# X's decays from half the lags, an immediate cosine bias, first steps of u in row pairs, and projections dealt over thirteen places a group

## The chip, the cores and the metric

The kernel runs as one program on one core of a Trainium2 chip. The metric is the device time of one execution in microseconds (us); for the kernel before it was taken three times. Below, PE is the matmul engine, ACT the scalar engine, DVE the vector engine, POOL the GpSimd engine, and SP the engine that issues most of the DMA transfers.

## The reference

Two branches over L = 2048 positions and D = 448 channels are mixed by a gate, all in f32.

```python
# A: a state space model's kernel of 2048 lags, applied to u as a convolution
dt = exp(log_dt);  A = -exp(log_A_real) + 1j * A_imag;  C = (C_real + 1j * C_imag) * dt
K = 2 * einsum("dn,dnl->dl", C, exp(A * dt * l)).real          # 256 states n, 2048 lags l
a = irfft(rfft(u, 2 * L) * rfft(K, 2 * L))[:L] + u * D_skip
# B: attention in 4 segments of 512 with a memory M, z; 16 heads of 28
q, k, v = x @ wq, x @ wk, x @ wv
for s in range(4):
    a_dot = softmax(q_s @ k_s.T * scale + mask) @ v_s
    a_mem = phi(q_s) @ M / (phi(q_s) @ z)
    o_s = sigmoid(beta) * a_mem + (1 - sigmoid(beta)) * a_dot
    M += phi(k_s).T @ v_s;  z += sum(phi(k_s))
b = concat(o) @ wo
out = g * a + (1 - g) * b,   g = sigmoid((x * gate_w).sum(-1)),  x = u
```

## The kernel before, in words

The program has three stretches: a preparation, a first half and a second half. The edit lies in the first two; the second half (attention, the Fourier steps, the output) keeps its instructions.

**Preparation** (`prepare_params`). The parameters lie as tiles of 112 rows (a quarter of the channels, four `j` side by side) by 256 states. Decay rates and phases are cut into three bf16 parts each (`parts`) and go to DRAM (SD, SP), from where `load_decay` and `load_phase` fetch them for four channels at a time into one of five tiles `lh`. `cab`, a factor of each channel and state, is brought with the states on the partitions by eight PE transposes.

**First half** (`first_half`). The kernel K is computed in 28 steps J of 16 channels, two steps to a *group*, so fourteen groups. A lag is split into a high part of 32 values and a low part of 64; the terms exp(-decay * lag) are therefore products of EX (high lags, 32 for each channel) and EY (low lags, 64 for each channel), and the same holds for the turning phases. For each J, `decay` makes three tiles: a pair of matmuls (two row halves of the array, one for each half of the states) writes the exponents to PSUM (`ps_arg`), and ACT takes the exponential of 1024 columns: two tiles EY and one EX. POOL then multiplies EX by `cab` (`scale`). For each half step n (four in a group), `turns(n)` writes the phases to PSUM with eight matmuls, `trig(n)` makes sine and cosine on ACT with three instructions (Sin, Abs, and Sin of the Abs with a bias of pi/2 read from the tile `bhp`), `product(n)` makes X and Y on DVE with four multiplications, and `sums(n)` contracts them with 64 small matmuls into `ps_k`. Sines and exponentials need different tables on ACT: each group has one table load ahead of its four sine blocks and one ahead of its decays. `decays(g + 1)` stands at the end of group g, and `sums` of a group's last half step is done within it.

**What is worked in between.** The class `Feed` holds a generator (`project`) of the projections q, k and v for branch B with their weight splits, stores and feature maps. The first half calls `feed.spend(us)` at five places: four lumps of `1.7 * RATES[g]`, one after each `trig(n)`, and after the tiles of `decays` by `PLACE` times `RATES[g]`. `spend` adds to a debt, at most 4.0, and takes steps from the generator until the debt is paid. When a step yields "pe", its products are held until the next decay, since their exponentials need that table: `exps` releases them ahead of a decay's exponential. A second generator, `transform_u`, does the first of the Fourier steps on u: 32 steps of one matmul on half of the rows (64), an eviction and a store. `project` takes steps from it (`filling`) at fixed places, and so does `spend` where a debt stays.

**The weight splits.** `weights` in `project` handles eight tiles of wq and wk (`win`): ACT copies the tile into the first half of a tile `wsp` as rounded values, POOL subtracts to get the rest, SP stores both to DRAM (WD). Two tiles `wsp` of their own are used in turn. A projection unit later fetches its weights from WD into a tile `w` (`load_w`), of which there are two.

The order of instructions on each engine follows from the program order of these calls and from a scheduler that simulates the engines; a change in one place can so shift others.

## Time and profile before

| | us |
|---|---|
| median of three runs | 871.44 |
| lowest and highest run | 870.67 and 874.49 |
| span of the profiled execution | 866.7 |
| preparation, up to the first table load for sines | 57.58 |
| first half, fourteen groups | 390.42 |
| second half | 418.70 |
| busy in the first half: PE, ACT, DVE, POOL | 347.50, 340.27, 295.22, 63.54 |

The page gives for the profiled execution its span alone, from the first to the last instruction; the times of the runs are a little longer than that span. The stretches are cut where ACT loads a table for a group's sines. The groups begin at 57.58, 89.28, 117.69, 144.63, 174.72, 200.49, 227.47, 254.69, 284.79, 310.56, 335.91, 363.23, 391.97 and 419.19 us, and the first score of the second half stands at about 448.

In the rows, a timeline's line gives the start, the duration, the engine, the line of the kernel, the operation, output<-inputs, the shape, how many instructions were joined (x), and in brackets the idle time before with what ended it. A window's line gives for each engine its busy time with its number of instructions, then the granted clock of PE (1.00 is full), the busy share of the DMA engines and GB/s. SPq is SP's DMA issue; line L1335 (L1337) is the helper through which most ACT instructions go, L1370 that of the matmuls.

### The profile page before, as it was taken

What the parts mean: (1) busy time and instruction counts of PE and PEld (TensorE: products, weight loads), DVE (VectorE), ACT (ScalarE), POOL (GpSimd) and SP (SyncE); (2) the same over time, 40 slices, a digit from 0 to 9 for tenths busy, and PEclk for the clock granted to TensorE, in tenths of its full rate; (3) what the DMA queues carried; (4) which work ended last, traced back from release to release, by engine and by line L of the source; (5) the groups of instructions that cost most, each with busy time, mean ns of one, the idle gap of its engine ahead of it and who ended that gap; (6) DMA issues with size and microseconds to landing.
All of it is one profiled execution on the core that took longest, in us unless ns stands there. A gap on an engine that the chain in (4) does not pass through costs nothing.

```text
span 866.7 us, 18996 instructions
## 1 busy us (share of the span) xinstructions
PE 753.7 (87%) x7575; PEld 410.3 (47%) x7597; DVE 596.9 (69%) x1160; ACT 539.2 (62%) x638; POOL 173.1 (20%) x217
## 2 busy tenths in 40 slices
PE   1687988998879988799979799999997998888997
PEld 1364655765547644476534444444443443343443
DVE  7988778777787777877648656656664747664564
ACT  4876989798997999979842255544453434431220
POOL 5224111001110011101100111222313124222110
PEclk9998999998999999999979689999999999878799
DMA  9347753334633255323569948557465545654873
GB/s 242 91 110 247 227 185 104 96 111 154 205 124 96 96 169 194 122 92 132 178 218 347 317 133 264 178 193 249 139 222 189 193 162 168 216 187 164 221 231 100
DMA packets 88290, 153.11 MB, mean 177 GB/s; under 512 B 20626, under 2 KB 57162, under 8 KB 88154
## 3 DMA queue, kind: packets, MB, share of 16 engines
q1 hardware_dynamic: 79130, 140.83, 50.2%
q10 hardware_dynamic: 7424, 9.18, 3.1%
q0 software_dynamic: 1648, 1.89, 0.7%
q8 instruction: 60, 0.98, 0.5%
q14 instruction: 28, 0.23, 0.1%
HBM read 90.87 MB, written 60.63 MB: 175 GB/s over the span
## 4 chain that ended last, share of the span: by engine, by line
PE 52%; ACT 16%; DVE 13%; issue 7%; DMA 7%; POOL 2%; SPq 1%; ACTq 0%; DVEq 0%; POOLq 0%
PE ps_a L1370 18%; PE ps_m L1370 16%; PE ps_pv L1370 7%; ACT cs L1335 7%; PE ps_arg L1370 4%; DVE jk L992 3%; PE ps_k L1370 3%; PE ps_m L1373 2%; ACT L1335 2%; DVE Y L397 2%; DMA WD<-wsp 1%; ACT EX L1335 1%; DMA dn<-pvs 1%; DVE Y L398 1%; DMA ident<-in_c_id 1%
## 5 line engine op out<-in xcount | busy, mean ns | idle before, releaser
L1023 ACT ACTIVATE PT<-ps_a 128x1024 f32<-128x1024 f32 (+1 forms) x96 | 84.5, 881 | 122.9 <-PE ps_a L1370 115.9
L992 DVE CUSTOM_DVE_ANT_0 jk<-ps_a,mk 128x512 f32<-128x512 f32 (+3 forms) x256 | 124.9, 488 | 49.6 <-PE ps_a L1370 42.3
L359 POOL TENSOR_TENSOR EX<-EX,cab 128x1024 f32<-128x1024 f32 x28 | 54.0, 1928 | 309.3 <-ACT EX L1335 286.3
L1335 ACT ACTIVATE cs<-ps_arg 128x1024 f32<-128x1024 f32 x111 | 107.3, 1021 | 2.7 <-DVE Y L398 2.4
L1370 PE MATMUL ps_a<-qu,ku 32*128 32x512 f32 (+3 forms) x768 | 92.9, 364 | 1.3 <-DVE mx L992 0.6
L1370 PE MATMUL ps_m<-xh,w 112*128 112x512 f32 x256 | 92.9, 412 | 0.7 <-DVE lo L762 0.5
L393 DVE TENSOR_TENSOR X<-EX,cs 128x1024 f32<-128x1024 f32 x56 | 70.5, 1260 | 23.2 <-ACT cs L1335 21.5
L1034 POOL TENSOR_SCALAR_AFFINE_SELECT PT<-PT 128x256 f32<-128x256 f32 (+1 forms) x96 | 47.1, 493 | 178.9 <-ACT PT L1023 178.7
L1370 PE MATMUL ps_k<-Y,X 128*32 128x64 f32 x3584 | 64.1, 226 | 11.8 <-DVE Y L398 11.8
L1370 PEld LDWEIGHTS ps_k<-Y,X 128*32 128x32 f32 x3584 | 54.9, 113 | 38.0 <-DVE Y L398 19.9
L397 DVE TENSOR_TENSOR Y<-EY,cs 128x1024 f32<-128x1024 f32 x56 | 70.0, 1251 | 0.0
L1370 PEld LDWEIGHTS ps_a<-qu,ku 32*128 32x128 f32 x768 | 64.8, 201 | 10.1 <-issue 3.2
L1335 ACT ACTIVATE cs<-cs,bhp 128x1024 f32<-128x1024 f32 x56 | 64.5, 1151 | 1.8
L1370 PE MATMUL ps_a<-ku,qu 32*128 32x512 f32 (+3 forms) x256 | 47.2, 404 | 16.0 <-DVE mx L992 8.4
L399 DVE SCALAR_TENSOR_TENSOR Y<-EY,cs 128x512 f32<-128x512 f32 x56 | 39.4, 704 | 30.5 <-ACT cs L1335 29.7
L1335 ACT ACTIVATE EY<-ps_arg 128x1024 f32<-128x1024 f32 x52 | 53.1, 1030 | 11.1 <-PE ps_arg L1370 10.0
L1370 PEld LDWEIGHTS ps_m<-xh,w 112*128 112x128 f32 x256 | 48.0, 188 | 20.0 <-issue 7.6
L1370 PEld LDWEIGHTS ps_a<-ku,qu 32*128 32x128 f32 x256 | 23.1, 195 | 62.7 <-issue 28.6
L1370 PE MATMUL ps_m<-xl,w 112*128 112x512 f32 x128 | 50.3, 393 | 0.0
L1370 PE MATMUL ps_arg<-ct,lh 64*128 64x512 bf16 x224 | 43.1, 386 | 8.1 <-ACT cs L1335 5.0
L1370 PEld LDWEIGHTS <-lh 64*128 64x128 bf16 x392 | 22.1, 95 | 50.6 <-issue 37.8
L604 DVE TENSOR_TENSOR pr<-ps_a,ks 128x896 f32<-128x896 f32 x32 | 34.7, 1085 | 15.7 <-PE ps_a L1370 15.4
(214 smaller groups left out, 1408.7 us busy)
## 6 DMA issues: line engine op xcount, KB each, us to landing
w<-WD SPq DMA_DIRECT2D x32, 448.0 KB
qu<-QD SPq DMA_DIRECT2D x16, 512.0 KB
ku<-KD SPq DMA_DIRECT2D x16, 512.0 KB
GU<-gs SPq DMA_DIRECT2D x32, 224.0 KB
GK<-gs SPq DMA_DIRECT2D x8, 896.0 KB
gk<-GK SPq DMA_DIRECT2D x32, 224.0 KB
gu<-GU SPq DMA_DIRECT2D x32, 224.0 KB
BB<-bs ACTq DMA_DIRECT2D x16, 448.0 KB
```

Source lines behind the costliest of these rows:

```text
L359: nc.gpsimd.tensor_tensor(o, o, cab, ALU.mult)
L393: v.tensor_tensor(X, ex, t[:, :, 0], ALU.mult)
L397: v.tensor_tensor(Y[:, :, :, :32], lo, y[:, :, :, ::-1], ALU.mult)
L398: v.tensor_tensor(Y[:, 0, :, 32:], ey[:, :, 32:], y[:, 0], ALU.mult)
L399: v.scalar_tensor_tensor(Y[:, 1, :, 32:], ey[:, :, 32:], -1.0, y[:, 1], ALU.mult, ALU.mult)
L604: nc.vector.tensor_tensor(pr[c], pt, ks.pop(c), ALU.mult)
L992: v.tensor_tensor_reduce(junk[:, :n], pt[:, x, o : o + n], k.mk[:, SEG - n :], 1.0, -3e38, ALU.add, ALU.max, mx[:, 3 - t, h : h + 1],)
L1023: nc.scalar.activation(PT[:, 2 * hp : 2 * hp + 2, 512 * b : 512 * b + n], pt[:, :, :n], AF.Exp, scale=SCALE)
L1034: nc.gpsimd.affine_select(sl, sl, pat, ALU.is_ge, 0.0, base=0, channel_multiplier=-1)
L1335: x = op(*args, **kw)
L1370: tc.keep_in_program_order(nc.tensor.matmul(*args, **kw))
L1373: tc.keep_in_program_order(nc.tensor.transpose(*args))
```

## The change

Five things are changed.

1. *X's decays.* `decay_x(J)` replaces two of the six `decay` calls of a group. It makes one tile ER for two steps J, from 16 high lags instead of 32 (256 columns for each J and half of the states), with four matmuls of 256 columns and one exponential of 1024. POOL's `scale` now writes EX from it in two multiplications of half the size: the first 16 lags are ER times `cab`, the other 16 are these times `gx` = exp(-1024 * decay). `gx` is prepared with eight transposes and two exponentials; so that the rates are still there, `parts` subtracts into a new tile `lr`. A group's decays start with `decay_x`, then come the four EY.
2. *Cosine's bias.* The bias pi/2 is an immediate instead of the tile `bhp`.
3. *u's first step.* When `k.pairs` is set, `transform_u` issues the two matmuls of a pair (upper and lower 64 rows) one after the other and then both evictions and stores.
4. *Dealing out.* `spend(g, share)` gives each of thirteen places of a group its share of `SHARES[g]`: five in the decays (PLACE) and eight in the sines (TRIG), two for each half step, one after `trig` and one after `sums`. The cap of 4.0 is gone, and releasing held exponentials no longer clears the debt. `FILLERS[g]` of u's steps, thirteen in all, are taken in pairs by a credit in `spend`; `project` takes none itself.
5. *Buffers.* The two tiles `wsp` now take the two buffers of the tag "w", which the tiles `w` use afterwards.

```diff
+    def decay_x(J):
+        pt = k.ps("arg")
+        for a in range(2):
+            for nt in range(2):
+                r, kw = rows(nt)
+                k.mm(
+                    pt[:, nt, 256 * a : 256 * a + 256], lt[J + a][r, 2], k.ce[r, 1024:],
+                    start=True, stop=True, **kw,
+                )
+        raw = gy.tile([128, 2, 2, 256], F32, tag="ER", name="ER", bufs=1)
+        exps(raw, pt)
+        for a in range(2):
+            EX[J + a] = raw[:, a]
+            if J > 0:
+                scale(J + a)
...
     def scale(J):
-        o = EX[J]
...
-            nc.gpsimd.tensor_tensor(o, o, cab, ALU.mult)
+        r = EX[J].rearrange("p t (d c) -> p t d c", c=16)
+        EX[J] = gy.tile([128, 2, 512], F32, tag="EX", name="EX", bufs=2)
+        o = EX[J].rearrange("p t (d c) -> p t d c", c=32)
+        lo, hi = 16 * J, 16 * J + 16
+        nc.gpsimd.tensor_tensor(o[:, :, :, :16], r, over(k.cab, lo, hi, 16), ALU.mult)
+        nc.gpsimd.tensor_tensor(o[:, :, :, 16:], o[:, :, :, :16], over(k.gx, lo, hi, 16), ALU.mult)
...
-        act(fl, fl, AF.Sin, bias=k.bhp, scale=-TWO_PI)
+        act(fl, fl, AF.Sin, bias=math.pi / 2, scale=-TWO_PI)
...
     def decays(g):
-        for J in (2 * g, 2 * g + 1):
-            for blk in range(3):
-                decay(J, blk)
-                if g > 0 and J % 2 and blk == 1:
-                    sums(4 * g - 1)
-                if g > 0:
-                    k.exps = 3 * (J % 2) + blk >= 2
-                    feed.spend(PLACE[3 * (J % 2) + blk] * RATES[g])
-                    k.exps = False
+        order = [(decay_x, (2 * g,))] + [(decay_y, (2 * g + a, blk)) for a in range(2) for blk in range(2)]
+        for i, (f, args) in enumerate(order):
+            f(*args)
+            if g > 0 and i == 3:
+                sums(4 * g - 1)
+            if g > 0:
+                k.exps = i >= 1
+                feed.spend(g, PLACE[i])
+                k.exps = False
...
         trig(n)
-        feed.spend(1.7 * RATES[n // 4])
+        feed.spend(n // 4, TRIG)
         product(n)
         if n == 2 * NJ - 1:
             feed.fill(2)
         if n % 4 > 0:
             sums(n - 1)
+        feed.spend(n // 4, TRIG)
...
-PLACE = (1.24, 0.62, 0.62, 0.62, 0.0, 0.62)
-RATES = (1.65, 1.65, 1.24, 1.55, 1.55, 1.17, 1.17, 1.48, 1.55, 1.17, 1.17, 1.48, 1.48, 1.65)
+PLACE = (0.9, 0.45, 0.45, 0.0, 0.45)
+TRIG = 0.5
+SHARES = (12.4, 11.6, 8.9, 15.2, 15.3, 8.1, 8.1, 14.5, 15.3, 8.1, 8.1, 14.5, 14.6, 12.8)
+FILLERS = (1, 0, 2, 0, 0, 2, 3, 0, 0, 2, 3, 0, 0, 0)
+SLOTS = sum(PLACE) + 8 * TRIG
...
-    def spend(self, us):
-        self.due = min(self.due + us, 4.0)
+    def spend(self, g, share):
+        part = share / SLOTS
+        self.due += SHARES[g] * part
+        self.credit += FILLERS[g] * part
         self.ends = False
         while self.due > 0 and not (self.held or self.done or self.ends and self.waiting):
             self.due -= self.step()
-        if self.due > 1.5 and (self.held or self.done) and self.waiting:
-            self.due -= next(self.filling, 0.0)
+        if self.credit > 0.99:
+            self.credit -= 1.0
+            self.k.pairs = True
+            next(self.filling, None)
+            self.k.pairs = False
     def exps(self):
         if self.held:
-            self.due = 0.0
             self.step()
...
-    wsp = [pp.tile([112, 4, 2, 4, 32], F32R, name=f"wsp{i}") for i in range(2)]
+    wsp = [
+        pp.tile([112, 4, 2, 128], F32R, tag="w", name="wsp", bufs=2).rearrange("p g b (j e) -> p g b j e", e=32)
+        for i in range(2)
+    ]
...
-    for _ in parts(k.SD, la, nc.gpsimd.tensor_tensor, k.pdma):
+    for _ in parts(k.SD, la, nc.gpsimd.tensor_tensor, k.pdma, new("lr", early)):
         pass
+    for nt in range(2):
...
+        nc.scalar.activation(by_j(k.gx[:, nt]), by_p(pt), AF.Exp, scale=-1024.0)
```

Three places of the programs show what the change moves. The first is ACT in group 0, from its table load on; `cs` are the sine tiles, `wsp` the copies of the weight splits, `win` their source. Before:

```order
L1337 ACT_TABLE_LOAD
L1337 ACTIVATE cs<-ps_arg 128x2x2x256
L1335 ACTIVATE cs<-ps_arg 128x2x2x256
L1335 ACTIVATE cs<-cs,bhp 128x1024
L1335 ACTIVATE wsp_212<-win 112x4x4x28
L1335 ACTIVATE cs<-ps_arg 128x2x2x256 x2
L1335 ACTIVATE cs<-cs,bhp 128x1024
L1335 ACTIVATE wsp_213<-win 112x4x4x28
L1335 ACTIVATE cs<-ps_arg 128x2x2x256 x2
L1335 ACTIVATE cs<-cs,bhp 128x1024
L1335 ACTIVATE wsp_212<-win 112x4x4x28
L1335 ACTIVATE cs<-ps_arg 128x2x2x256 x2
```

And now:

```order
L1378 ACT_TABLE_LOAD
L1378 ACTIVATE cs<-ps_arg 128x2x2x256
L1376 ACTIVATE cs<-ps_arg 128x2x2x256
L1376 ACTIVATE cs<-cs 128x1024
L1376 ACTIVATE wsp<-win 112x4x4x28 x2
L1376 ACTIVATE cs<-ps_arg 128x2x2x256 x2
L1376 ACTIVATE cs<-cs 128x1024
L1376 ACTIVATE wsp<-win 112x4x4x28 x2
L1376 ACTIVATE cs<-ps_arg 128x2x2x256 x2
L1376 ACTIVATE cs<-cs 128x1024
L1376 ACTIVATE wsp<-win 112x4x4x28 x2
L1376 ACTIVATE cs<-ps_arg 128x2x2x256 x2
```

The copies of group 0 stood one after each sine block, with the rest behind the table load for the decays; now they stand in pairs after the first, second and third block.

The second place is SP's queue in the same group, where `WD` is the DRAM tensor of the split weights and `w` a projection unit's weight tile. Before:

```order
L1394 DMA WD<-wsp_212 112x4x256
L1394 DMA win<-in_B_wk 112x448
L1394 DMA WD<-wsp_213 112x4x256
L1394 DMA win<-in_B_wk 112x448
L733 DMA w<-WD 112x1024 x2
L1394 DMA WD<-wsp_212 112x4x256
L328 DMA lh_91<-SP 48x2x128 x2
L1394 DMA WD<-wsp_213 112x4x256
```

And now:

```order
L1436 DMA WD<-wsp 112x4x256
L1436 DMA win<-in_B_wk 112x448
L1436 DMA WD<-wsp 112x4x256
L1436 DMA win<-in_B_wk 112x448
L1436 DMA WD<-wsp 112x4x256
L334 DMA lh_90<-SP 48x2x128 x2
L1436 DMA WD<-wsp 112x4x256 x3
L779 DMA w<-WD 112x1024 x3
```

The first two loads of `w` stood between the fourth and the fifth store of the splits; now all loads stand behind the eighth.

The third place is ACT from the table load for the decays in group 3 (it makes the decays of group 4), where `e` and `hi` are what was held of the projections. Before:

```order
L1335 ACT_TABLE_LOAD
L1335 ACTIVATE e<-ps_m 128x512
L1335 ACTIVATE hi<-ps_m 128x512
L1335 ACTIVATE e<-ps_m 128x512
L1335 ACTIVATE hi<-ps_m,po 128x512
L1335 ACTIVATE EY<-ps_arg 128x1024
L1335 ACTIVATE v_207<-ps_m 128x16x28
L1335 ACTIVATE EY<-ps_arg 128x1024
L1335 ACTIVATE EX<-ps_arg 128x1024
L1335 ACTIVATE EY<-ps_arg 128x1024 x2
L1335 ACTIVATE EX<-ps_arg 128x1024
```

And now:

```order
L1376 ACT_TABLE_LOAD
L1376 ACTIVATE ER<-ps_arg 128x2x2x256
L1376 ACTIVATE e<-ps_m 128x512
L1376 ACTIVATE hi<-ps_m 128x512
L1376 ACTIVATE e<-ps_m 128x512
L1376 ACTIVATE hi<-ps_m,po 128x512
L1376 ACTIVATE EY<-ps_arg 128x1024 x4
```

The two EX have become one ER, and it has moved from among the EY to the head of the decays, ahead of the held exponentials.

More of the change, by code (lines that the diff above doesn't have):

```diff
@@ L523, in transform_u @@
     uts = {0: load(0), 1: load(1)}
[L524 to L528 removed]
+    todo = [(w, h) for w in range(16) for h in range(2)]
+    while todo:
+        n = 2 if k.pairs and todo[0][1] == 0 else 1
+        now, todo = todo[:n], todo[n:]
+        pts = []
+        for w, h in now:
+            if h == 0 and w < 14:
+                uts[w + 2] = load(w + 2)
             pt = k.ps("m")
[L530 to L533 removed]
+            r = slice(64 * h, 64 * h + 64)
+            k.mm(pt[:, :D], k.s1u[r], uts[w][r], start=True, stop=True)
+            pts.append(pt)
+        for (w, h), pt in zip(now, pts):
             gs = up.tile([128, D], F32, tag="gs", name="gs", bufs=3)
@@ L1346, in gated_mix @@
     k.exps = False
+    k.pairs = False
     def copy(out, x, f, **kw):
```

90 lines of the change are left out of this document (39 added, 51 removed).

## The prediction

> **What bounds the kernel now.** I read the busy times first, then the span cut at the points where ScalarE (ACT) loads the table for a group's sines, then the timeline of single groups. Busy times of the page first, then groups 0, 1, 3, 9, 10 and 13 with the sum over all fourteen:
>
> ```profile
> PE 753.7 (87%) x7575; PEld 410.3 (47%) x7597; DVE 596.9 (69%) x1160; ACT 539.2 (62%) x638; POOL 173.1 (20%) x217
> ...
> core 0: us, PE busy (x) PEld busy (x) DVE busy (x) ACT busy (x) POOL busy (x), PEclk, DMA share, GB/s
> 57.58:89.28 31.70, 23.87 (x355) 13.97 (x358) 24.81 (x23) 23.70 (x26) 15.73 (x9) 0.89 0.76 226
> 89.28:117.69 28.41, 27.37 (x374) 17.60 (x372) 22.50 (x30) 24.08 (x26) 3.83 (x2) 1.00 0.75 246
> 144.63:174.72 30.09, 28.27 (x390) 20.06 (x387) 20.28 (x31) 24.48 (x28) 3.83 (x2) 1.00 0.24 73
> 310.56:335.91 25.35, 22.02 (x346) 13.17 (x346) 19.98 (x27) 24.43 (x28) 3.82 (x2) 1.00 0.51 171
> 335.91:363.23 27.32, 22.04 (x344) 13.07 (x345) 22.54 (x32) 26.00 (x32) 3.83 (x2) 0.94 0.42 141
> 419.19:448.00 28.81, 23.74 (x330) 12.38 (x329) 19.32 (x29) 19.51 (x25) 1.91 (x1) 0.89 0.45 157
> sum 390.42, PE 347.50 PEld 218.64 DVE 295.22 ACT 340.27 POOL 63.54; mean PE 24.82 PEld 15.62 DVE 21.09 ACT 24.31 POOL 4.54
> ```
>
> The whole-span shares hide the stage that is edited. The fourteen groups fill 57.58 to 448.00, 390.4 us of 866.7, and what follows them is the same program before and after. Taking group 0 and group 13 off the sum leaves twelve groups (89.28 to 419.19, 329.9 us) with PE busy 347.50 - 23.87 - 23.74 = 299.9 and ACT busy 340.27 - 23.70 - 19.51 = 297.1. So a group lasts 27.5, holds 25.0 of PE and 24.8 of ACT, and neither has more than 2.7 to spare. The rows show two kinds: 144.63 has PE at 28.27 of 30.09 while ACT waits, and 310.56 and 335.91 have ACT at 24.43 of 25.35 and 26.00 of 27.32 while PE waits. Group 0 is of a third kind: no engine is full, and it lasts 31.7.
>
> **The change, part by part.** *X's decays.* In each group two EX exponentials become one. The form rows of two tiles, a stretch of PE's timeline with a pair of decay products, and two rows of ACT's:
>
> ```profile
> L359 POOL TENSOR_TENSOR EX<-EX,cab x28: 1910/1912/2357, 60.0 to 419.2; 128x1024 f32<-128x1024 f32 x28
> L1335 ACT ACTIVATE EX<-ps_arg x26: 1007/1024/1032, 83.8 to 418.1; 128x1024 f32<-128x1024 f32 x26
> ...
> 163.15 0.39 PE L1370 MATMUL ps_arg<-ce,lh 64*128 64x512 bf16 x2
> 163.47 0.47 PE L1370 MATMUL ps_m<-wvh,xh 112*128 112x450 f32 x1
> ...
> 29.94 1.15 ACT L211 ACTIVATE pin_c<-pin_g,bhp 112x1024 f32<-112x1024 f32 x1
> 31.00 1.04 ACT L211 ACTIVATE pin_b<-pin_g 112x1024 f32<-112x1024 f32 x1
> ```
>
> ACT loses one exponential of 1.02, about 0.93 in a row of them since neighbours overlap by about 0.1 (29.94 + 1.15 against a next start at 31.00). PE loses half of two pairs of 512 columns; a pair holds PE from 163.15 to 163.47, so 0.32 a group. POOL does two multiplications of half the size for one of 1.91: the same 3.8 a group, or up to 4.5 if the halves carry a fixed cost.
>
> *Cosine's bias.* The same function on the same shape takes 1.15 with a bias tile and 1.04 without. Four cosines a group: 0.4 of ACT.
>
> *u's first step in pairs.* Two steps use the upper and lower 64 rows of the array.
>
> ```profile
> 123.73 1.02 PE L1370 MATMUL ps_m<-ut,s1u 64*128 64x448 f32 x2
> ```
>
> One step is two passes in 1.02, the last 0.2 of it overlapping what follows, so 0.8. The pair of decays above shows two row halves running in the time of one. Thirteen pairs in thirteen groups would give 0.8 each; some of the old steps already ran beside a decay's other half, so I take 0.65, with bounds 0 and 0.9.
>
> *The dealing.* In groups 1 to 12, then, ACT loses 0.93 + 0.4 = 1.3 and PE 0.32 + 0.65 = 1.0. A group ends by the later of two nearly equal engines, so the gain is about 1.0 to 1.3 if the 2.5 us of mutual waiting stay. Spreading the projections over eight places in the sines instead of four should take something off that waiting. Against it stands the new place of X's decay: it is the first exponential of a group, and PE reaches it only behind the third sums and a slice of projection. One group's decays in the timeline today:
>
> ```profile
> 217.57 1.28 ACT L1335 ACT_TABLE_LOAD   x1
> ...
> 217.88 1.10 PE L1370 MATMUL ps_k<-Y,X 128*32 128x64 f32 x64
> ...
> 218.87 0.60 ACT L1335 ACTIVATE e<-ps_m 128x512 f32<-128x512 f32 x1
> ```
>
> Today ACT fills that gap with the held exponentials (e at 218.87, right after the table load). Afterwards ACT waits for sums (to 218.9), about 0.7 of projection and 0.3 of decay: to 219.9, 1.0 late, which costs only where ACT is the bound. I take 1.25 a group net, -15 for twelve; bounds -2 (the waits only move) and -27 (1.3 and another 1.0 of waiting gone).
>
> *Group 0.* Six of the eight q and k weight splits fall here. Each goes ACT copy, POOL subtraction, store to DRAM, and a tile is free for its next copy when its store has landed. Now the copies go out in pairs after each sine block, and the tiles that the projections read their weights into share the two buffers of the splits. From the timeline and the waits of group 0, in this order: ACT's copies, the DMAs, SP's issue of a load, POOL, PE.
>
> ```profile
> 62.57 0.56 ACT L1335 ACTIVATE wsp<-win 112x448 fp32r<-112x448 f32 x1
> 66.04 0.56 ACT L1335 ACTIVATE wsp<-win 112x448 fp32r<-112x448 f32 x1
> 72.21 0.58 ACT L1335 ACTIVATE wsp<-win 112x448 fp32r<-112x448 f32 x1
> ...
> 74.72 1.15 ACT L1335 ACTIVATE cs<-cs,bhp 128x1024 f32<-128x1024 f32 x1
> ...
> 80.98 0.58 ACT L1335 ACTIVATE wsp<-win 112x448 fp32r<-112x448 f32 x1 [1.66 <-DMA WD<-wsp]
> ...
> 68.70 5.85 DMA WD<-wsp
> 77.85 4.95 DMA WD<-wsp
> 85.60 5.53 DMA w<-WD
> ...
> 74.57 0.79 SPq L733 DMA_DIRECT2D w<-WD  x2
> ...
> 64.15 2.11 POOL L721 TENSOR_TENSOR wsp<-win,wsp 112x448 fp32r<-112x448 f32 x1
> ...
> 84.01 1.15 POOL L721 TENSOR_TENSOR wsp<-win,wsp 112x448 fp32r<-112x448 f32 x1 [1.22 <-ACT wsp L1335]
> ...
> 80.81 0.59 PE L1370 MATMUL ps_m<-xh,w 112*128 112x512 f32 x1
> ...
> 90.53 0.38 PE L1370 MATMUL ps_arg<-ct,lh 64*128 64x512 bf16 x2
> ```
>
> The fourth split's store lands at 68.70 + 5.85 = 74.55, and POOL's subtractions keep it from coming much earlier. Before, ACT ran the third sine block (from 69) while that was under way. After, the fifth and sixth copies stand ahead of that block, so it starts at 75.1 and ends at 78. The seventh copy waits for the fifth's store (copy 0.6, subtraction 1.15 to 2.1, store 5 to 5.5: about 79.5), the eighth for the sixth's (82). The fourth block then ends at 85.4; it ended at 74.72 + 1.15 = 75.9. Worse, the first weight load may now start only when the seventh store has landed: 79.5 + 0.6 + 1.2 + 0.2 + 5 = 86.5, and arrives 5.5 later, at 92. Before, that load left at 74.57 and PE used it at 80.81. The new order puts this unit ahead of the third sums, X's decay and all that follows on PE, so all of these wait until 92. From its first product PE needed 90.9 - 80.8 = 10.1 to the end of the next group's first turns; now it has one block of sums (1.0) and six more products (1.4) in that stretch: 12.5. PE will have stood idle for over 10 us, and the trace shows what follows such a stop, one row of the timeline and two of the windows around it:
>
> ```profile
> 68.92 1.94 PE L1370 MATMUL ps_k<-Y,X 128*32 128x64 f32 x64 [5.60 <-DVE Y L398]
> ...
> 66.00:70.00 4.00, 1.07 (x41) 1.08 (x45) 4.00 (x4) 1.63 (x4) 1.90 (x2) 0.54 1.04 356
> 70.00:74.00 4.00, 3.66 (x72) 1.73 (x67) 4.00 (x5) 3.84 (x5) 1.14 (x1) 0.61 0.87 260
> ```
>
> After 5.6 us of idling the granted clock is 0.54 and 0.61, and the sums take 1.94 instead of 1.10. I add 1.3 for this: 105.8 against 90.9, or +14.9, less the 1.4 of products done ahead: +13.5. I take +13, with bounds +5 (stores and loads of 4 us on a quieter DMA) and +17. The Trainium skill (TensorE: Matmul & The Clock Gate, "What's actually happening") has the clock at half for about 3.4 us of activity after an idle window; by that the restart would cost 1.7, not 1.3, and the sum would be 0.4 higher. The two rows agree with it in kind.
>
> *Ahead of and behind the groups.* The new exp(-1024 lambda) adds one table load and two exponentials to ACT in the preparation, and eight transposes to PE.
>
> ```profile
> 28.06 0.58 ACT L1356 ACTIVATE wvh<-winv 112x448 fp32r<-112x448 f32 x1 [1.01 <-DMA winv<-in_B_wv]
> ```
>
> That is 1.28 + about 1.1 on ACT; 1.0 of it fits into the idle time before 28.06, and one exponential less in group 0's decays gives back 0.93. Net +0.5 (0 to +1.5). Group 13 has four shorter cosines and one u step less in its tail, which waits on ACT and stores: -2 (0 to -3).
>
> The sum against the profiled execution: 866.7 + 0.5 + 13 - 15 - 2 = 863.2. The page gives this execution's span only; the median of the three runs, 871.44, lies 4.7 above it, which I carry over: 868, by 3.4 us faster. About 0.5%, 4.4 us, is what a measurement of this kernel can tell from no change.
>
> **Rivals.** *DVE becomes the bound (slower).* POOL's four multiplications now run straight after the first exponential of the decays, when DVE multiplies the fourth X and Y, from two SBUF operands each. Before, they ran late in the decays and under the next table load.
>
> ```profile
> 59.96 4.23 POOL L359 TENSOR_TENSOR EX<-EX,cab 128x1024 f32<-128x1024 f32 x2 [22.95 <-DVE cab L211]
> ...
> 62.76 2.50 DVE L393 TENSOR_TENSOR X<-EX,cs 128x1024 f32<-128x1024 f32 x1 [0.35 <-ACT cs L1335]
> ...
> 69.39 1.21 DVE L393 TENSOR_TENSOR X<-EX,cs 128x1024 f32<-128x1024 f32 x1
> ```
>
> Beside POOL the same multiplication took 2.50 instead of 1.21. If each group loses 1 to 2 us of DVE so, then the sums behind that product are late, and with them the last decays. It decides where DVE has less than about 2 to spare in the decays; 335.91 has 22.54 of 27.32 for its whole group, so I think the slack mostly holds it. Price: 1 us in twelve groups, 868 + 12 = 880, slower. The Trainium skill (SBUF — State Buffer, "Who interferes with whom") says that a VectorE instruction with two SBUF inputs and a GpSimd one that reads SBUF exclude each other for a whole instruction; the 2.50 agrees.
>
> *The even dealing does more (faster).* If another 1.0 of the 2.5 of waiting goes in each of twelve groups: 868 - 12 = 856. For it: 144.63 has ACT idle for 5.6 us, and projection bursts there hold PE. Against it: 310.56 is within 0.9 of ACT's own time already.
>
> *The pairs don't pair.* Two steps need two free PSUM buffers of three, two of which units may hold. Then 13 x 0.65 = 8.5 of PE stays, of which PE-bound groups feel about 6: 874.
>
> **How the numbers follow.** The forecast, 868 with its own range 862 to 874, has 0.40; the lucky dealing 0.27; the DVE bound 0.25; no pairing 0.08. Faster by over 0.5% is below 867.1: 0.17 of the forecast and all of the dealing, 0.44. Slower is above 875.8: 0.23 of the DVE bound and 0.02 each of forecast and pairing, 0.27. The rest, 0.29, is within 0.5%. The range reaches into both outer cases: 851 (dealing, with group 0 at its lower bound) to 883.
>
> **What would show it.** Group 0, from its table load to the next group's, should last 43 to 47 instead of 31.7, with a PE wait for w of over 8 us near 80 to 92 and ACT waits for WD stores before the fifth to eighth copies. Groups 1 to 12 should last about 26.2 on average, with 23.4 of ACT and 24.0 of PE in each. The cosine should take 1.05, and a pair of u steps about as long as one. I am wrong if group 0 stays near 32, if the twelve groups save less than 5 us together, or if DVE's X and Y in the decays last far over 1.2.

## The result and the profile after

The changed kernel takes 950.12 us (median of 4 runs, 941.77 to 955.15) against 871.06 for the kernel before (4 runs, 865.82 to 874.49): a ratio of 1.0887, 95% interval 1.0806 to 1.0969. The forecast was 868, with a range of 851 to 883. The profiled execution has a span of 940.1, and its run took 941.77. Here and in the experiments medians are of all runs, and ratios leave out slow runs, those over 1.5% above the fastest of the same kernel.

The busy times of the page, after:

```profile
PE 780.1 (83%) x7584; PEld 420.0 (45%) x7605; DVE 609.3 (65%) x1161; ACT 521.0 (55%) x625; POOL 182.6 (19%) x245
```

ACT has 18 us less to do, as the change says, and the span is 73.4 longer. The windows cut at the table loads for sines show where (groups 0, 1, 4, 6 and 9 and the first part of 13; columns as before):

```profile
59.00:106.35 47.35, 28.15 (x357) 15.87 (x358) 24.55 (x23) 22.96 (x26) 18.92 (x14) 0.75 0.60 173
106.35:135.11 28.76, 25.87 (x363) 14.95 (x362) 19.88 (x26) 22.25 (x26) 4.11 (x4) 1.00 0.60 187
199.60:232.31 32.71, 28.72 (x370) 17.34 (x369) 21.80 (x30) 22.82 (x26) 4.29 (x4) 0.90 0.40 128
265.19:303.52 38.33, 29.31 (x353) 16.50 (x349) 24.21 (x33) 24.33 (x30) 4.47 (x4) 0.78 0.35 117
370.10:400.15 30.05, 23.72 (x350) 12.89 (x348) 19.63 (x25) 23.99 (x29) 4.29 (x4) 0.94 0.45 147
496.14:521.00 24.86, 23.27 (x335) 12.36 (x331) 19.00 (x23) 18.22 (x22) 2.12 (x2) 1.00 0.48 169
```

Group 0 lasts 47.35 instead of 31.70 (+15.65). Groups 1 to 12 last 496.14 - 106.35 = 389.8 instead of 329.9 (+59.9). The preparation is 1.4 longer, group 13 and the second half together 3.6 shorter. These make the 73.4.

The loss of groups 1 to 12 has two parts. One window over all twelve, before and after:

```profile
89.28:419.19 329.91, 299.89 (x4343) 192.29 (x4340) 251.09 (x350) 297.06 (x338) 45.90 (x24) 0.97 0.44 143
...
106.35:496.14 389.79, 323.95 (x4338) 198.92 (x4338) 261.85 (x347) 278.50 (x323) 52.98 (x48) 0.91 0.36 117
```

PE idles 65.8 us instead of 30.0. It is also busy 24 us longer for practically the same matmuls (4338 and 4343 in the trace), at a mean granted clock of 0.91 instead of 0.97. So some 36 of the 60 us are waiting and some 24 are slower matmuls. How a stop of PE is followed by a low clock is shown at the end.

A group has two stretches: the sines, from the table load for sines to that for the decays, and the decays. Here are the sums of the windows over groups 1 to 12, first the sines and then the decays; before:

```profile
sum 184.06, PE 165.45 PEld 108.58 DVE 138.14 ACT 177.36 POOL 22.94; mean PE 13.79 PEld 9.05 DVE 11.51 ACT 14.78 POOL 1.91
...
sum 145.85, PE 134.44 PEld 83.71 DVE 112.94 ACT 119.70 POOL 22.96; mean PE 11.20 PEld 6.98 DVE 9.41 ACT 9.98 POOL 1.91
```

and after:

```profile
sum 253.86, PE 216.44 PEld 133.94 DVE 174.03 ACT 177.88 POOL 0.00; mean PE 18.04 PEld 11.16 DVE 14.50 ACT 14.82 POOL 0.00
...
sum 135.93, PE 107.51 PEld 64.98 DVE 87.82 ACT 100.61 POOL 52.98; mean PE 8.96 PEld 5.42 DVE 7.32 ACT 8.38 POOL 4.42
```

Before, ACT worked 177.36 of the 184.06 us of the sines: it set their pace. After, it works as long (177.88) in 253.86. The decays became 10 shorter, the sines 70 longer. The waits of ACT and of PE over groups 1 to 12, after:

```profile
ACT EY L1376 <- PE ps_arg L1412: 31.6, 20, 4.6
ACT L1376 <- PE ps_arg L1412: 30.6, 11, 4.4
ACT gs L1376 <- PE ps_m L1412: 22.6, 13, 4.7
ACT v L1376 <- PE ps_m L1412: 10.6, 5, 4.7
ACT am L1376 <- PE ps_m L1412: 7.0, 4, 2.9
...
PE ps_k L1412 <- DVE Y L426: 18.6, 13, 2.9
```

and before, the same view:

```profile
ACT EY L1335 <- PE ps_arg L1370: 8.2, 15, 1.6
ACT v L1335 <- PE ps_m L1370: 6.9, 6, 1.6
ACT gs L1335 <- PE ps_m L1370: 1.6, 2, 0.9
...
PE ps_k L1370 <- DVE Y L398: 4.9, 5, 1.2
```

The columns are total wait, number of waits and longest. All of these waits of ACT are for PE (the second line is the table load for the decays, behind which X's decay comes first), and PE waits for DVE's Y ahead of the sums.

Group 6 of the changed kernel shows how a wait looks in the timeline:

```profile
278.05 1.06 ACT L1376 ACTIVATE cs<-cs 128x1024 f32<-128x1024 f32 x1
...
282.43 1.34 PE L1412 MATMUL ps_m<-ut,s1u 64*128 64x448 f32 x2 [1.93 <-DVE tm L853]
283.80 0.54 ACT L1376 ACTIVATE gs<-ps_m 128x448 f32<-128x448 f32 x1 [4.69 <-PE ps_m L1412]
284.40 1.86 PE L1412 MATMUL ps_m<-ut,s1u 64*128 64x448 f32 x2 [0.63 <-ACT gs L1376]
...
286.29 0.54 ACT L1376 ACTIVATE gs<-ps_m 128x448 f32<-128x448 f32 x1 [1.95 <-PE ps_m L1412]
286.73 1.94 ACT L1376 ACTIVATE cs<-ps_arg 128x1024 f32<-128x1024 f32 x2
```

A pair of u's steps stands between two sine blocks. Its first product waits for DVE (tm), its second for the first eviction (gs); that each wait is for a PSUM buffer is read from the program, not from these rows. ACT, in program order, stands still for 4.69 and 1.95 before the next sines. It is not a pair in time either: 282.43 and 284.40 are apart by a whole step.

### The profile page after: what moved, and what is told of

It reads as the page before. It is cut to its first block, busy times and chain, and to the rows that moved or that the text cites. A ratio compares the mean times of both kernels' runs of the same rounds, so it can differ in the third digit from the quotient of the medians.

```text
span 940.1 us, 19033 instructions
## 1 busy us (share of the span) xinstructions
PE 780.1 (83%) x7584; PEld 420.0 (45%) x7605; DVE 609.3 (65%) x1161; ACT 521.0 (55%) x625; POOL 182.6 (19%) x245
## 4 chain that ended last, share of the span: by engine, by line
PE 52%; ACT 15%; DVE 15%; issue 7%; DMA 7%; SPq 2%; POOL 1%; ACTq 0%; DVEq 0%; POOLq 0%
PE ps_m L1412 18%; PE ps_a L1412 17%; PE ps_pv L1412 7%; ACT cs L1376 6%; PE ps_k L1412 5%; PE ps_arg L1412 3%; DVE jk L1033 3%; DVE Y L425 2%; PE ps_m L1415 2%; ACT L1376 2%; DVE X L420 1%; DMA WD<-wsp 1%; DVE Y L426 1%; DVE e L822 1%; ACT ER L1376 1%
## 5 line engine op out<-in xcount | busy, mean ns | idle before, releaser
L1412 PE MATMUL ps_m<-xh,w 112*128 112x512 f32 x256 | 106.9, 451 | 17.7 <-DMA w<-WD 13.5
L375 POOL TENSOR_TENSOR EX<-ER,cab 128x512 f32<-128x512 f32 x28 | 30.9, 1125 | 371.9 <-ACT ER L1376 350.6
L1412 PE MATMUL ps_k<-Y,X 128*32 128x64 f32 x3584 | 70.1, 237 | 24.8 <-DVE Y L426 24.6
L1412 PEld LDWEIGHTS ps_k<-Y,X 128*32 128x32 f32 x3584 | 60.3, 121 | 46.5 <-DVE Y L426 33.4
L1412 PEld LDWEIGHTS ps_m<-xh,w 112*128 112x128 f32 x256 | 51.1, 200 | 47.4 <-issue 29.8
L1376 ACT ACTIVATE cs<-cs 128x1024 f32<-128x1024 f32 x56 | 59.2, 1058 | 1.8
L1412 PE MATMUL ps_m<-xl,w 112*128 112x512 f32 x128 | 53.0, 414 | 0.0
L1376 ACT ACT_TABLE_LOAD x27 | 34.6, 1283 | 30.9 <-PE ps_arg L1412 30.6
L1412 PE MATMUL ps_arg<-ct,lh 64*128 64x512 bf16 x224 | 45.8, 396 | 3.3 <-ACT cs L1376 1.9
```

Of the source, the lines that this page charges most:

```text
L375: nc.gpsimd.tensor_tensor(o[:, :, :, :16], r, over(k.cab, lo, hi, 16), ALU.mult)
L1376: x = op(*args, **kw)
L1412: tc.keep_in_program_order(nc.tensor.matmul(*args, **kw))
```

## The experiments

Times are medians; the ratio is to runs of the kernel before on the same chip. That kernel's own medians lie between 866.6 and 871.1 in these series, so a loss is taken against the kernel before of the same series: 79 us for the changed kernel. Groups and waits are those of the profiled executions. In the edits, what stands behind # is a remark, and ... marks lines left out.

**1. Undo the dealing in the changed kernel.**

```diff
-                feed.spend(g, PLACE[i])          # and TRIG after trig and after sums
+                feed.spend(PLACE[i] * RATES[g])  # and 1.7 * RATES after trig alone
...
+        self.due = min(self.due + us, 4.0)       # cap, clearing and filling as before
```

> The changed kernel with the dealing of before: lumps of 1.7 * RATES after each sine block, PLACE * RATES in the decays (1.24, 0.93, 0.93, 0, 0.62 over the five tiles, the same 3.72 in all), the cap of 4.0, the debt cleared at a release, u's steps taken singly by the projections. X's decay at the head, the immediate bias and the split tiles in the buffers of w stay. Theory D (the dealing: slices behind the sums and evictions put among the sines make the sine stretch last 21 instead of 15): groups 1 to 12 come back to 27 on average, their sine stretches to 15 to 16, total 870 to 885, of which up to 10 is group 0. Theory X (X's decay at the head: the table load and the first exponential wait for a product that stands behind the third sums): the idle time of ACT ahead of that load stays at 2 to 3 a group, total 905 to 925. Theory P (u's pairs): pairs are gone here too, so 920 to 930 if they alone were at fault and the slices were not.

Measured: 884.4, ratio 1.0169 (1.0116 to 1.0223). Theory D holds in the total and in the mean of groups 1 to 12 (327.6, or 27.3 each): 64 of the 79 go with the dealing. It does not hold in the parts: the sine stretches last 18.4 on average instead of 15 to 16, and group 0 lasts 44.7, 13 longer than in the kernel before.

**2. No pairs.**

```diff
-            self.k.pairs = True
             next(self.filling, None)
-            self.k.pairs = False
+            next(self.filling, None)
```

> The changed kernel with each pair of u's steps taken as two single steps at the same place; all else as changed. Theory P (the pairs' second step waits for a PSUM buffer, and two evictions in a row hold ACT between sine blocks): ACT's 22.6 of waiting before gs mostly goes, total 920 to 930. Theory D (the dealing as such): two single steps at the same place wait as a pair does, within 10 of the changed kernel, 938 to 955.

Measured: 942.5, ratio 1.0819 (1.0763 to 1.0876). The interval overlaps that of the changed kernel, and ACT still waits 24.3 for gs (22.6 with pairs). That two steps are issued as a pair is not what costs.

**3. The shared buffers alone, in the kernel before.**

```diff
-    wsp = [pp.tile([112, 4, 2, 4, 32], F32R, name=f"wsp{i}") for i in range(2)]
+    wsp = [
+        pp.tile([112, 4, 2, 128], F32R, tag="w", name="wsp", bufs=2).rearrange("p g b (j e) -> p g b j e", e=32)
+        for i in range(2)
+    ]
```

> The kernel before with one part alone: the split tiles take the buffers of the weight tiles. The prediction's step on group 0: the first load of w waits for the store of the seventh split, so PE gets its first weights some 8 to 10 later; here the copies are not bunched, so group 0 lasts 37 to 41 instead of 31.7 and the total is 876 to 881. Rival (the stores land in time and other work fills PE meanwhile): 870 to 873.

Measured: 879.8, ratio 1.0104 (1.0049 to 1.0159); group 0 lasts 42.2, a little over what was expected, and groups 1 to 12 stay (329.7). This is the prediction's mechanism, without the bunching of the copies.

**4. The dealing alone, in the kernel before.**

```diff
-        feed.spend(1.7 * RATES[n // 4])
+        feed.spend(n // 4, TRIG)      # again after sums; SHARES, FILLERS, spend and exps as in the change
```

> The kernel before with the new dealing alone (thirteen places, SHARES, no cap, no clearing, u's steps in pairs by credit); six decays as before, with 0.9, 0, 0.45, 0.45, 0, 0.45 behind them, bias tile and split tiles of their own. Theory D: the sine stretches grow to 19 to 21 as in the changed kernel, total 920 to 945. Theory X: the dealing costs little without X's decay at the head, 870 to 890. Theory P: the pairs' waits are here too, 890 to 905.

Measured: 928.3, ratio 1.0684 (1.0633 to 1.0734), as theory D has it; the sine stretches last 18.5 on average. With 1: the dealing costs 59 by itself and 64 in the changed kernel.

**5. The dealing with u's steps as before** (kernel of 4).

```diff
-        if self.credit > 0.99:        # two steps of u by credit
+            yield -next(filling, 0.1) # one step at the projections' own places
```

> The kernel before with the thirteen places and SHARES, but u's first steps taken singly by the projections as before, not in pairs by credit. It stands against the dealing alone (928.3). Theory F (where u's pairs fall: among the sines, with both evictions on ACT, which waited 27.6 for them): 893 to 905. Theory S (the slices of projection, not u's steps, stretch the sines): 918 to 930.

Measured: 937.9, ratio 1.0823 (1.0750 to 1.0897). It does not answer the question. SHARES have no room for u's steps, and projections were left over: from the last group's start to the second half's first matmul 68 us pass, against 29 in the kernel before. Groups 1 to 12 take 348.9 where 4 took 383.7, but with 4192 matmuls in them instead of 4338.

**6. One lump a half step** (kernel of 4).

```diff
-        feed.spend(n // 4, TRIG)      # after trig
+        feed.spend(n // 4, 2 * TRIG)
...
-        feed.spend(n // 4, TRIG)      # after sums
```

> The kernel before with the new dealing, but each half step's two slices in one place, behind the sine block; the second one behind the sums is gone, the amounts are the same. It stands against the dealing alone (928.3). Theory R (the ring: a slice behind the sums delays the next turns, which ACT waits for): 890 to 905, sine stretches of 16 to 17. Theory S (the amount among the sines, 64% of a group's share, is more than PE can do beside turns and sums in 15): 920 to 930.

Measured: 894.6, ratio 1.0327 (1.0259 to 1.0394). Theory R holds: taking the slice from behind the sums to ahead of them, with the same amounts, gives back 33 of 59. In groups 1 to 12 it is 29.5 (354.2 against 383.7, with 4341 and 4338 matmuls): PE idles 17.5 less and is busy 11.9 less, at a mean granted clock of 0.95 against 0.92. The waits of PE suggest how. With the slice behind the sums (kernel of 4, from 95 to 475 us):

```profile
PE ps_k L1381 <- DVE Y L398: 21.6, 14, 2.9
```

With one lump (kernel of 6, from 100 to 450 us):

```profile
PE ps_k L1380 <- DVE Y L398: 1.7, 2, 1.1
```

The lump ahead of the sums is what PE does while DVE makes Y. Half of it is not enough cover: PE stands idle at the sums, and does the other half when the next turns and the evictions are already wanted. This is a reading of the waits. A wait for Y is not a loss in itself: in the kernel of 17 PE waits 13.8 for Y, and groups 1 to 12 last no longer than in the kernel before.

**7. Cap and clearing** (kernel of 4).

```diff
-        self.due += SHARES[g] * part
+        self.due = min(self.due + SHARES[g] * part, 4.0)
...
+            self.due = 0.0            # at a release
```

> The kernel before with the new dealing, but the debt capped at 4.0 and cleared when held products are released. It stands against the dealing alone (928.3). Theory B (debt that piles up while products are held is spent in a burst in the decays, ahead of the products of EY, for which ACT waited 34): 900 to 912, decays of the groups with shares of 15.3 at 11 instead of 13.5 to 14.7. Otherwise 922 to 932.

Measured: 934.6, ratio 1.0781 (1.0711 to 1.0852), above both expectations. As in 5, what is cleared is left over to the end (68 us from the last group's start). It doesn't tell whether bursts cost.

**8. X's decay third, with the dealing of before.**

```diff
+        order = order[1:3] + order[:1] + order[3:]
```

> The first experiment's kernel (dealing of before, all else as changed, 884.4) with X's decay third in the decays, behind two EY. Theory X (the first place costs: 15.6 of ACT's waiting ahead of the table load, because the product stands behind the third sums and a slice on PE): the wait goes, 870 to 875. Rival (the wait moves to the first EY, whose product stands behind the same work, or POOL's multiplications end too late for the next group's first X): 882 to 888.

Measured: 880.5, ratio 1.0155 (1.0098 to 1.0212), against 1.0169 in 1: not apart, and between the two expectations. The wait moves, as the rival says: ACT waits 15.6 ahead of the table load in 1 and not at all here, but its wait for EY's products grows from 6.8 to 18.7.

**9. One lump in the changed kernel.** The edit is that of 6.

> The changed kernel with one edit: each half step's two slices in one place behind the sine block, none behind the sums. Theory R (a slice behind the sums delays the next turns, for which ACT waits, and the wait goes round by DVE's products to the next sums): as much comes back as in the kernel before with the dealing, 28 to 38 of the 79, so 912 to 922. Theory S (in the changed kernel the wait stands elsewhere: X's decay at the head, group 0): under 15 comes back, 935 to 950.

Measured: 907.4, ratio 1.0488 (1.0417 to 1.0559). The loss is 41 instead of 79, so 38 come back, the upper end of what theory R gave. Groups 1 to 12 go from 389.8 to 359.7, and most of PE's wait for Y goes too:

```profile
PE ps_k L1411 <- DVE Y L426: 3.5, 4, 1.1
```

**10. The immediate bias alone.**

```diff
-        act(fl, fl, AF.Sin, bias=k.bhp, scale=-TWO_PI)
+        act(fl, fl, AF.Sin, bias=math.pi / 2, scale=-TWO_PI)
```

> The kernel before with the cosine's immediate bias alone, 0.1 less on ACT in each of 56 cosines. The prediction's step: 0.4 a group where ACT bounds, 2.5 to 5 less. Rival (a sine block is paced by DVE's four multiplications, 3.7 a block, and ACT's 3.0 hides behind them): within 1.5 of before.

Measured: 865.3 (12 runs) against 866.6 (17 runs), ratio 0.9982 (0.9951 to 1.0013). The sum over the sines of groups 1 to 12:

```profile
sum 179.62, PE 159.85 PEld 105.06 DVE 136.06 ACT 172.94 POOL 22.95; mean PE 13.32 PEld 8.75 DVE 11.34 ACT 14.41 POOL 1.91
```

That is 4.4 less than 184.06, 0.37 a group where 0.4 was worked out; ten of the twelve groups save 0.2 to 0.4. So ACT paces the sines, and the rival's DVE does not. The whole time cannot tell the two apart.

**11. The lumps cut in two, nothing else, in the kernel before.**

```diff
-        feed.spend(1.7 * RATES[n // 4])
+        feed.spend(0.85 * RATES[n // 4])
...
             sums(n - 1)
+        feed.spend(0.85 * RATES[n // 4])
```

> The kernel before with one edit: each lump of 1.7 * RATES is cut in two halves, one behind the sine block as before and one behind the sums; amounts, cap, clearing and u's steps as before. Theory R (the ring): slower by 20 to 40, 889 to 909, sine stretches of 17 to 20. Theory S: within 8 of before.

Measured: 896.8, ratio 1.0338 (1.0275 to 1.0401), 30 slower, as theory R has it. But only 16 of it are lost in groups 1 to 12; 13 are lost in group 0, where the copies now come in pairs and wait for stores. So the slice behind the sums costs with the old amounts too, about half of what it costs with the new ones.

**12. One lump, u's steps as before.** The edits of 5 and 6 together.

> The kernel before with the new dealing in one lump a half step (894.6) and u's steps taken singly by the projections as before. Theory F2 (with the ring's slice gone, what is left of the loss is u's pairs, for whose evictions ACT waited 15.2 and which the five groups that hold them pay with 18): 872 to 880. Rival (the rest is SHARES and the uncleared debt): 888 to 896.

Measured: 925.0, ratio 1.0690 (1.0616 to 1.0763). Again 68 us pass from the last group's start to the second half, so the total answers nothing; groups 1 to 12 take 341.1 against 354.2 in 6, but with 4195 matmuls instead of 4341.

**13. The second slice evicted by DVE, in the changed kernel.**

```diff
+        k.exps = True
         feed.spend(n // 4, TRIG)      # after sums
+        k.exps = False
```

> The changed kernel with one edit: what the slice behind the sums evicts from PSUM goes to DVE instead of ACT; the slice stays where it is. Theory E (ACT, which works in program order, waits for that slice's evictions, and the slice waits on PE for sums, so for DVE, so for ACT's own cosine): ACT's 46 of waiting for v, gs, am and pkT in groups 1 to 12 goes for the most part, total 905 to 925. Theory T (the slice delays the next turns on PE, wherever it is evicted): 938 to 955.

Measured: 967.6, ratio 1.1160 (1.1100 to 1.1220). Theory E falls, and the time is above theory T's range too. The waits of ACT over groups 1 to 12:

```profile
ACT L1378 <- PE ps_arg L1414: 70.6, 12, 12.0
ACT EY L1378 <- PE ps_arg L1414: 33.6, 24, 4.5
ACT cs L1378 <- PE ps_arg L1414: 14.6, 7, 5.1
ACT v L1378 <- PE ps_m L1414: 7.6, 2, 4.2
```

ACT's waiting for v, gs, am and pkT falls from 46.0 to 19.9, but what it waits for PE's exponents and phases (ps_arg) grows from 62.4 to 118.8. PE in turn now waits 24.7 for evictions of pkT, gs and am on DVE. So taking the evictions off ACT does not help. That PE's order alone costs, wherever the slice is evicted, is not shown by this run, since the edit also loads DVE.

**14. u's pairs only in the decays** (one lump, kernel of 6).

```diff
-        if self.credit > 0.99:
+        if self.credit > 0.99 and self.k.exps:
```

> The kernel before with the new dealing in one lump (894.6), and u's pairs taken only in the decays, where they are evicted by DVE. Theory F3 (the five groups that hold the pairs lost 18 of the 25 that are left, with 15.2 of ACT's waiting for gs among the sines): 874 to 882. Rival (amounts): 889 to 898.

Measured: 900.4, ratio 1.0395 (1.0333 to 1.0457), above both expectations. F3 falls as it was put. The sums of sines and decays over groups 1 to 12 show why:

```profile
sum 186.27, PE 161.45 PEld 105.77 DVE 139.33 ACT 174.52 POOL 22.95; mean PE 13.45 PEld 8.81 DVE 11.61 ACT 14.54 POOL 1.91
...
sum 173.19, PE 155.95 PEld 90.80 DVE 126.63 ACT 111.27 POOL 22.96; mean PE 13.00 PEld 7.57 DVE 10.55 ACT 9.27 POOL 1.91
```

The sines are nearly as short as in the kernel before (186 against 184), the decays 27 longer. Against 6 the sines lost 18 and the decays gained 24: the pairs' price moved with them. The five groups with pairs last 22.5 longer than in the kernel before, the seven others 7.0; in 6 it was 18.2 and 6.1.

**15. More in the decays** (kernel of 6).

```diff
-PLACE = (0.9, 0.0, 0.45, 0.45, 0.0, 0.45)
+PLACE = (1.8, 0.0, 0.9, 0.9, 0.0, 0.9)
...
-TRIG = 0.5
+TRIG = 0.25
```

> The kernel before with the new dealing in one lump (894.6), with 69% of a group's share in the decays instead of 36% (PLACE doubled, half the lump in each half step). Theory A (what is left of the loss is that PE gets more projection among the sines than fits beside turns and sums, while ACT is full there): 872 to 882, sine stretches of 15 to 15.5. Rival (bursts ahead of EY's products make ACT wait in the decays instead): 890 to 905.

Measured: 943.0, ratio 1.0885 (1.0816 to 1.0953). Theory A falls; the rival's direction holds, and far over its price: over groups 1 to 12 the decays grow from 149.6 in 6 to 189.7, and the sines stay at 207.7 (204.7).

**16. Three edits in the changed kernel** (6, 14 and 8).

> The changed kernel with three edits together: one lump a half step, u's pairs only in the decays, X's decay third. If the parts add up (907.4 for the lump, about 12 for the pairs, 4 for the place of X's decay): 886 to 896; if the places interact, 900 to 910.

Measured: 898.7, ratio 1.0328 (1.0249 to 1.0407): 47 of the 79 come back, 9 more than with the lump alone. It lies between the two expectations. The parts do not add up as measured singly: the 12 expected of the pairs was not what 14 measured, where taking them in the decays made the kernel of 6 no faster.

**17. SHARES with room for u's steps** (kernel of 12).

```diff
-SHARES = (12.4, 11.6, 8.9, 15.2, 15.3, 8.1, 8.1, 14.5, 15.3, 8.1, 8.1, 14.5, 14.6, 12.8)
+SHARES = (14.2, 11.6, 12.5, 15.2, 15.3, 11.7, 13.5, 14.5, 15.3, 11.7, 13.5, 14.5, 14.6, 12.8)
```

> The kernel before with the new dealing in one lump, u's steps taken singly by the projections as before, and SHARES raised by what these steps are charged (1.8 a pair: 14.2, 11.6, 12.5, 15.2, 15.3, 11.7, 13.5, 14.5, 15.3, 11.7, 13.5, 14.5, 14.6, 12.8). In it the two units of a group are ready when the decays begin, so their held exponentials stand right behind the table load in every group, as in the kernel before. Theory H (the rest of the dealing's loss comes from units that get ready only within the decays: their release stands behind one to three exponentials, two of three PSUM buffers stay taken and PE, in order, waits ahead of EY's products): 868 to 880. Rival (the thirteen places cost by themselves): 888 to 900.

Measured: 875.5 (10 runs), ratio 1.0082 (1.0045 to 1.0120), in theory H's range. With one lump, u's steps where the projections take them and SHARES to suit, the loss of the dealing is 7 instead of 59. In the profiled run, which took 881.8, groups 1 to 12 last 329.6 with 4340 matmuls, as in the kernel before (329.9 with 4343); group 0 lasts 38.2 instead of 31.7. So what is left of the loss does not stand in groups 1 to 12. Theory H's order is not what the trace has, though: in groups 1 to 5 an EY is still ahead of the held exponentials, and these five together last as long as before (138.3 against 138.2).

**18. More in the sines** (kernel of 6).

```diff
-PLACE = (0.9, 0.0, 0.45, 0.45, 0.0, 0.45)
+PLACE = (0.45, 0.0, 0.22, 0.22, 0.0, 0.22)
...
-TRIG = 0.5
+TRIG = 0.75
```

> The kernel before with the new dealing in one lump and u's pairs by credit (894.6), with 84% of a group's share in the sines instead of 64% (TRIG 0.75; PLACE 0.45, 0, 0.22, 0.22, 0, 0.22). The held exponentials stand right behind the table load again, u's pairs stay among the sines. Theory H: 872 to 884. Theory F (u's pairs are the rest, for whose evictions ACT waited 15.2): 888 to 898. Theory A (PE gets more among the sines than fits): 900 to 915.

Measured: 914.5 (the three runs of the ratio have a median of 909.3), ratio 1.0503 (1.0410 to 1.0596), in theory A's range. Theory H falls: here the held exponentials stand right behind the table load in all twelve groups, and it is 15 slower than 6. What 17 and 18 differ in is u's steps and the amounts. ACT waits 32.8 for gs here, 15.2 in 6 and 0.8 in 17. Theory A cannot be the whole account, since 15, with less among the sines, was slower still.

## Why the prediction was wrong, point by point

*Group 0: right, and a little short.* The forecast was 43 to 47, measured 47.35. The steps are in the timeline, ACT's copies, SP's stores and loads, and PE's first product with its weights:

```profile
74.92 0.58 ACT L1376 ACTIVATE wsp<-win 112x448 fp32r<-112x448 f32 x1 [6.09 <-DMA WD<-wsp]
77.84 0.58 ACT L1376 ACTIVATE wsp<-win 112x448 fp32r<-112x448 f32 x1 [2.35 <-DMA WD<-wsp]
...
79.66 6.40 SPq L1436 DMA_DIRECT2D WD<-wsp  x3
86.97 13.13 SPq L779 DMA_DIRECT2D w<-WD  x3
...
92.06 0.76 PE L1412 MATMUL ps_m<-xh,w 112*128 112x512 f32 x1 [13.51 <-DMA w<-WD]
...
94.89 1.94 PE L1412 MATMUL ps_k<-Y,X 128*32 128x64 f32 x64
```

The fifth and the sixth copy (the third and fourth of this group) wait 6.09 and 2.35 for stores of earlier splits, the first load goes behind the eighth store at 86.97, and PE gets weights at 92.06. The working had 92, but on the clock of the kernel before, whose group 0 starts 1.4 earlier; counted from the group's start PE got its weights 1.4 sooner than worked out, and the rest of the group took 14.3 where 13.8 was worked out. Experiment 3 has the buffers' part of it alone, +10.5 in group 0. The term of +13, bounds +5 and +17, measured +15.65.

*Groups 1 to 12: the step that failed.* "So the gain is about 1.0 to 1.3 if the 2.5 us of mutual waiting stay. Spreading the projections over eight places in the sines instead of four should take something off that waiting." The term of -15 measured +59.9. The step took the place of the projections as neutral or better, with nothing for a slice behind the sums. The 2.5 of waiting was read as slack of a whole group, but ACT paced the sines (177.36 of 184.06), and PE's lumps lay where it would otherwise wait for Y. Experiments 6, 9 and 11 show what half a lump behind the sums costs in three kernels: 33, 38 and 30 in all, and 29.5, 30.1 and 16.2 in groups 1 to 12. The prediction followed the order of ACT and SP, and on PE that of group 0 and of the slice ahead of X's decay; the second slice of the other half steps it did not price. Nor did it count that PE, where it waits more, is also granted a lower clock: about 24 of the 60 us.

*u's steps: no gain, and part of the loss.* The pairs were counted as a gain of 0.65 each. Undoing them changes nothing that the runs can tell (2). The rival saw that two steps need two PSUM buffers of three, but priced only the lost pairing. With one lump left, the dealing still costs 26; with u's steps at the projections' own places and SHARES to suit it costs 7 (17). That is 19 us, shown for the two edits together and not for each. It isn't the pairing (2), and taking the steps out of the sines does not help (14). That the steps wait for buffers that the units hold, as in the timeline of group 6, is the likely reason, since ACT's wait for gs goes with the loss (32.8, 15.2 and 0.8 in 18, 6 and 17); it was not tried by itself. Why more in the sines (18) and more in the decays (15) cost 15 and 50 more than 6 stays open.

*X's decays and the bias: sizes right, little gained.* The cosine takes 1.06 and a group has one exponential less, as said. Most of the term of -15 rested on them. Yet the changed kernel with the old dealing (1) lies 4.6 above the shared buffers alone (3), intervals overlapping, and its groups 1 to 12 take 327.6 against 329.7: 2 less. ACT has 14.7 less to do in them than in the kernel before, but idles 12.4 longer. The late place of X's decay, put at 1.0 a group where ACT is the bound, is part of this: the table load waits 15.6 for it in 1 and 30.6 in the changed kernel, though in 8 such a wait only moved. The sums of 1 over sines and decays:

```profile
sum 220.44, PE 189.33 PEld 123.04 DVE 180.18 ACT 182.35 POOL 0.00; mean PE 15.78 PEld 10.25 DVE 15.01 ACT 15.20 POOL 0.00
...
sum 107.17, PE 103.88 PEld 65.86 DVE 71.65 ACT 100.04 POOL 51.47; mean PE 8.66 PEld 5.49 DVE 5.97 ACT 8.34 POOL 4.29
```

The decays fell by 39 and the sines rose by 36. DVE's work moved by as much, from 113 to 72 in the decays and from 138 to 180 in the sines. Part of this is the cut alone, since the table load that ends the sines now waits for X's decay. What DVE used to do beside the exponentials may now run against the products of X and Y; that this is the reason is not shown.

*The rivals.* DVE's products were not slowed by POOL. The rows of X and of POOL's first multiplication after the change (least, median and largest ns of one):

```profile
L420 DVE TENSOR_TENSOR X<-EX,cs x56: 1211/1224/2065, 64.9 to 514.1; 128x1024 f32<-128x1024 f32 x56
L375 POOL TENSOR_TENSOR EX<-ER,cab x28: 1057/1061/1444, 61.4 to 490.0; 128x512 f32<-128x512 f32 x28
```

X's median stays at 1.22 us. In groups 1 to 12 the 48 X take 58.7 together against 58.6 before, and the 144 Y 124.4 against 124.1. The rival's condition hardly arose: only one of these 192 ran at the same time as a multiplication of POOL. The rival that the even dealing does more, 856, had the sign wrong. No rival priced a slice behind the sums. The lower end of the range does not follow from its parts: 856 with group 0 at +5 instead of +13 gives 848, not 851; the upper end, 883, has no sum.

## What to carry to other kernels

Filler work, work put in where an engine would wait, has a place and not only an amount. Laid ahead of an instruction that must wait, it costs little as far as the wait covers it; laid behind it, it delays whatever comes next in that engine's order. Here half of the same work behind the sums cost 29.5 and 30.1 us in two kernels. Before moving it, read for each stretch which engine is full and what the filler covers there; a group's mean hides both. When an edit leaves an engine waiting, also read its granted clock: here 24 of 60 us were slower matmuls. A table of amounts must include all that is to be done, or the rest is paid at the end (5, 7 and 12). That filler which needs buffers of a shared pool belongs where the pool is free is likely from 17, and not shown by itself.

## What the hardware did that was not expected

After 13.5 us of PE idling in group 0, the clock stayed at half for over 6 us of full work. The windows of the changed kernel there:

```profile
92.00:94.00 2.00, 1.94 (x5) 1.58 (x6) 0.00 (x0) 0.00 (x0) 0.00 (x0) 0.50 0.08 27
94.00:96.00 2.00, 2.00 (x47) 1.35 (x49) 0.00 (x0) 0.00 (x0) 0.00 (x0) 0.50 0.00 0
96.00:98.00 2.00, 2.00 (x35) 1.42 (x27) 0.00 (x0) 0.00 (x0) 0.00 (x0) 0.50 0.03 8
98.00:100.00 2.00, 2.00 (x10) 0.71 (x9) 0.00 (x0) 1.08 (x2) 0.00 (x0) 0.83 0.00 0
```

From 92.06 to about 98.7 it is 0.50 (a mean of 0.83 in the last window would be 0.7 us at half and the rest at full clock), so 6.6 us. The 64 sums that start at 94.89 take 1.94 us; those at 76.05, before the stop, took 1.10. The Trainium skill (TensorE: Matmul & The Clock Gate, "What's actually happening") has the full clock back after at least one busy window of about 3.4 us, and says that the windows run freely and do not start with the work. The 6.6 us here are almost two such windows. At half clock they lose an estimated 3.3 us, half of 6.6, where the prediction put 1.3 for the restart.
